# One attention and channel-mix kernel: every engine's order set by hand in place of a scheduler's, with a new start

## The chip, the cores and the metric

The kernel runs on one core of one Trainium2 chip. The profile lists five engines: PE with the matmuls and transposes (1324 instructions in the changed kernel), DVE (385), ACT (229), POOL (57), and SP, for which it shows nothing but transfers being issued. The program gives each engine its own queue of instructions, and the profile tells what an engine waited for. The metric is device time in microseconds (us) of one execution; the executions of one kernel lie within 0.3 to 1.4% of each other. A profiled execution gives a trace; its span, from the first to the last instruction, is about 1.8 us shorter than the time.

## The reference, cut to what matters

```python
# 8 batches, 8 heads, 576 rows, 64 columns a head; C = 512, F = 1024
q_s = softmax(q, over the 64 columns); k_s = softmax(k, over the 576 rows)
kv  = einsum('bhsd,bhse->bhde', k_s, v)
x   = einsum('bhsd,bhde->bhse', q_s, kv)          # to (batch, 576, 512)
x_prev = x shifted by one row
xk = mu_k * x + (1 - mu_k) * x_prev
xr = mu_r * x + (1 - mu_r) * x_prev
out = sigmoid(xr @ w_r) * (relu(xk @ w_k)**2 @ w_v)
```

## The kernel before: the parts that matter

Attention is made per batch in two groups of four heads, so there are 16 groups. The parts of a group, with the names that the profile uses:

```python
exp(i)        # ACT: eqk <- raw, exp of q (i=0) and of k (i=1)
cast_v        # ACT: vv <- raw
norm_q        # DVE: rsum <- eqk, rrec, qs <- eqk * rrec          (about 3.0 us)
kv, weights   # PE: kvp <- vv, eqk;  DVE: rz, w <- kvp * rz
transpose_q   # PE: qtp <- qs, 9 transposes
copy_qt       # ACT: qt <- qtp
x(0), x(1)    # PE: xp <- qt, w;  ACT: xb <- xp
diff          # DVE: xb (first rows), xd
mix(0), mix(1)# DVE: xm, xk;  xm, xr                               (1.4 us each)
```

The two layers are made per pair of batches (1152 rows) in three units of 512, 384 and 256 rows: `kfp` (PE) -> `rel` (ACT) -> square `k` or `k2` (DVE), then per 128 rows `rp` (PE) -> `th` (ACT) and `vp` (PE) -> `ot` (DVE) -> store. A unit can begin only when xk of its last batch is there.

Only the start (batch 0) had its order by hand. From then on a generator laid out attention pieces between matmul groups, and the framework's scheduler put the instructions of PE, ACT and DVE in order:

```python
for pair in range(B // 2):
    for c0, n in UNITS:
        advance(ASTEPS * (2 * pair + (c0 + n - 1) // S))
        for c in unit(pair, c0, n, 4 if pair == 0 and c0 == 0 else 1):
            cols += c
            advance(min((B - 1) * ASTEPS, ASTEPS * (cols + per_batch // 8) // per_batch))
```

The softmax here doesn't subtract the row's maximum and nothing guards it: scores larger than these inputs give would overflow.

Of the kernel before, what the change touches and what calls it, by code (L numbers as in the profile page):

```python
# [18 lines left out]
def kernel(  # L19
# [42 lines left out]
    ctx.enter_context(tc.manual_schedule(engines={mybir.EngineType.Pool}))  # L62

    def emit_load(b: int, g: int, queues=None):
        t = ldpool.tile([128, 3, 2, J * D], F32, tag="raw", name="raw")
        ld = []
        for i, src in enumerate((q, k, v)):
            ap = bass.AP(tensor=src.tensor,
                         offset=src.offset + (b * H + 2 * g) * S * D,
                         ap=[[J * D, 128], [4 * S * D, 2], [1, J * D]])  # L70
            queue = queues[i] if queues else nc.gpsimd
            ld.append(queue.dma_start(out=t[:, i, :, :], in_=ap))  # L72
        raw[b, g] = t
        return ld

    first = emit_load(0, 0, (nc.sync, nc.scalar, nc.sync))
# [5 lines left out]
    emit_load(0, 1, (nc.scalar, nc.sync, nc.scalar))  # L82
# [4 lines left out]

    ident = const.tile([128, 128], BF16, name="ident")
# [20 lines left out]
    def emit_weights(gate):  # L109
# [11 lines left out]
        for u in range(2):  # L121
            part(wr_bf, moe_w_r, C, u, 0, C)
        n = FT // 2
# [16 lines left out]

    class Attention:
        def __init__(self, b: int, g: int):
            self.b, self.g = b, g
            self.t = raw.pop((b, g))
# [8 lines left out]
        def exp(self, i: int):  # L153
            nc.scalar.activation(  # L154
                out=self.eqk[:, i, :, :, :],
                in_=self.t[:, i, :, :].rearrange("p u (j d) -> p j u d", d=D),
                func=ACT.Exp)
# [5 lines left out]
        def norm_q(self):  # L163
# [3 lines left out]
            rrec = apool.tile([128, 2 * J], F32, tag="rrec", name="rrec")  # L167
            nc.vector.reciprocal(out=rrec[:], in_=rsum[:])
# [3 lines left out]
                in1=rrec[:, :, None].to_broadcast((128, 2 * J, D)), op=ALU.mult)  # L172

        def kv(self, tag: str):
# [3 lines left out]
            else:  # L178
                self.kvp = [psum.tile([128, 512], F32, tag="mm", bufs=4, name="kvp")[:, :]
                            for _ in range(2)]  # L180
            for j in range(J):
# [27 lines left out]
        def x(self, hf: int):  # L209
            self.xp = psum.tile([128, 1024], F32, tag="att", bufs=2, name="xp")  # L210
            for c, e in ((0, 8), (8, J)):
                nc.tensor.matmul(self.xp[:, 64 * c:64 * e], lhsT=self.w[:, hf, :],  # L212
                                 rhs=self.qt[:, c:e, 64 * hf:64 * hf + 64],
                                 start=True, stop=True)
            nc.scalar.copy(out=self.xb[:, hf, 64:64 + S], in_=self.xp[:, 0:S])  # L215
# [20 lines left out]
    def attention(b: int, g: int):  # L236
        a = Attention(b, g)
        a.exp(0)
        a.exp(1)
        a.cast_v(nc.scalar.copy)  # L240
        a.norm_q()
        yield
        a.kv("att")
        a.weights()
        yield
        a.transpose_q()
        a.copy_qt()
        yield
        a.x(0)
        yield  # L250
        a.x(1)
        yield
        a.diff()
        a.mix(0)
        yield
        a.mix(1)
        yield


    def unit(pair: int, c0: int, n: int, step: int = 1):  # L260
        xk, xr = xpair[pair]
        k2 = mpool.tile([128, FT, 512], BF16, tag="k2", name="k2")
        for f0 in range(0, FT, step):
            kfps = [psum.tile([128, 512], F32, tag="mm", bufs=4, name="kfp")
                    for _ in range(step)]
            for cts in ((0, 1), (2, 3)) if step > 1 else (range(CT),):
                for i, kfp in enumerate(kfps):
                    fc = f0 + i
                    for ct in cts:
                        nc.tensor.matmul(kfp[:, 0:n],  # L270
                                         lhsT=wk_bf[:, ct, fc * 128:(fc + 1) * 128],
                                         rhs=xk[:, ct, c0:c0 + n],
                                         start=(ct == 0), stop=(ct == CT - 1))
            for i, kfp in enumerate(kfps):
                rel = mpool.tile([128, 512], BF16, tag="rel", bufs=3, name="rel")
                nc.scalar.activation(out=rel[:, 0:n], in_=kfp[:, 0:n], func=ACT.Relu,  # L276
                                     scale=HALF_ROOT)
                nc.vector.tensor_tensor(out=k2[:, f0 + i, 0:n], in0=rel[:, 0:n],
                                        in1=rel[:, 0:n], op=ALU.mult)
                yield n  # L280
        for m in range(n // 128):
            rp = psum.tile([128, C], F32, tag="mm", bufs=4, name="rp")
# [3 lines left out]
            th = mpool.tile([128, C], F32, tag="th", name="th")  # L286
            nc.scalar.activation(out=th[:], in_=rp[:], func=ACT.Tanh, scale=0.5)  # L287
            yield 512
            vp = psum.tile([128, C], F32, tag="mm", bufs=4, name="vp")
            for ft in range(FT):  # L290
                nc.tensor.matmul(vp[:], lhsT=k2[:, ft, 128 * m:128 * m + 128],  # L291
                                 rhs=wv_bf[:, ft, :], start=(ft == 0), stop=(ft == FT - 1))
            ot = opool.tile([128, C], F32, tag="ot", name="ot")
            nc.vector.scalar_tensor_tensor(out=ot[:], in0=th[:], scalar=1.0, in1=vp[:],  # L294
                                           op0=ALU.add, op1=ALU.mult)
            for i in range(2):
# [7 lines left out]
    def drain(gen):  # L304
        for _ in gen:
            pass
# [93 lines left out]
```

## Time and profile before

| | before |
|---|---|
| time, median of 3 (range) | 221.39 us (220.98 to 221.61) |
| span of the profiled execution | 219.7 us |
| first kfp that run through from | 27.82 us |
| ten periods between the groups' transposes, 6th to 16th | 118.9 us, 11.89 each |

The first view gives busy times in stretches of the span. The columns are PE, weight loads, DVE, ACT, POOL, each with its count of instructions, then the granted PE clock (1.00 is full), the share of DMA time, and GB/s. Where the trace has no clock record the clock column is 1.00 too; in this kernel the first record is at 24.27 us, so before that the column tells nothing.

```profile
core 0: us, PE busy (x) PEld busy (x) DVE busy (x) ACT busy (x) POOL busy (x), PEclk, DMA share, GB/s
0.00:28.00 28.00, 9.96 (x72) 5.98 (x73) 12.96 (x38) 12.52 (x14) 11.33 (x22) 0.99 1.03 250
28.00:60.00 32.00, 30.12 (x210) 14.88 (x209) 31.25 (x68) 31.05 (x45) 13.17 (x19) 0.95 1.03 398
60.00:200.00 140.00, 138.25 (x949) 72.53 (x948) 116.33 (x268) 98.49 (x161) 11.30 (x16) 1.00 0.44 140
```

In the first 28 us PE stands 18 us. From 28 to 60 us DVE and ACT are full (31.25 and 31.05 of 32 us). From 60 to 200 us PE is idle for 1.75 of 140 us. The list of waits of PE says for what it stood:

```profile
engine line waited for: us in total, times, longest us
PE mup L134 <- DMA mu_sb<-in_moe_mu_r_dram: 9.8, 1, 9.8
PE kfp L270 <- DVE xk L232: 3.7, 2, 2.9
...
PE kvp L184 <- ACT vv_107 L160: 2.1, 1, 2.1
PE qtp L202 <- DVE qs L170: 1.5, 1, 1.5
...
```

And the timeline shows where the start ends: kfp begin at 20.80 us on the half of xk that is ready, stop, and run on only from 27.82 us. Those at 20.80 us start 0.43 us apart, where 0.22 us is usual from 60 us on: PE ran at half rate there. (Start, duration, engine, line, operation, tile; in brackets the idle time before and what ended it.)

```profile
20.80 2.77 PE L270 MATMUL kfp<-xk,wk_bf 128*128 128x512 bf16 x6
...
24.30 0.59 PE L270 MATMUL kfp<-xk,wk_bf 128*128 128x512 bf16 x2
27.82 2.72 PE L270 MATMUL kfp<-xk,wk_bf 128*128 128x512 bf16 x6 [2.92 <-DVE xk L232]
```

### The profile page before, as it was taken

Reading aid. Unit: us, or ns where it says so; the run is one execution under the profiler, and the core shown is the slowest. Engines: PE = TensorE matmul, PEld = TensorE weight load, DVE = VectorE, ACT = ScalarE, POOL = GpSimd, SP = SyncE. Lnnn points to the kernel's source line nnn. Section 1 sums busy time; section 2 is a strip of 40 time slices with the busy share of each in tenths; the row PEclk is TensorE's granted clock in tenths of the full one; section 3 lists DMA queues with packets and bytes.
Section 4 is the critical chain, followed back from the end, with each engine's and each line's share of the span. In section 5 each row is a group of like instructions: output and inputs, shape, how many; then the busy total and the mean of one; then the engine's idle time right before and its main releaser. Section 6 shows DMA issues by size and latency. Waiting matters only on the chain.

```text
span 219.7 us, 3641 instructions
## 1 busy us (share of the span) xinstructions
PE 193.5 (88%) x1313; PEld 101.6 (46%) x1313; DVE 166.3 (76%) x384; ACT 147.7 (67%) x230; POOL 35.8 (16%) x56
## 2 busy tenths in 40 slices
PE   0156599988999999999999999999999999999991
PEld 0134134534547454445557443546465444554650
DVE  1196389999999998889798998888787758483431
ACT  2645279999977779676929696949736392644340
POOL 1294252433431210230030000000000000000000
PEclk9999969999999999999999999999999999999999
DMA  6999999999999791897085220232131400340414
GB/s 215 397 158 199 262 402 388 393 400 403 404 393 406 273 343 71 256 298 288 3 264 201 49 51 0 57 90 48 36 88 24 95 3 22 73 95 5 108 36 95
DMA packets 16171, 40.62 MB, mean 185 GB/s; under 512 B 2072, under 2 KB 4632, under 8 KB 16152
## 3 DMA queue, kind: packets, MB, share of 16 engines
q0 software_dynamic: 8736, 27.40, 38.0%
q1 hardware_dynamic: 6600, 11.22, 18.0%
q10 hardware_dynamic: 816, 1.77, 2.2%
q8 instruction: 10, 0.16, 0.3%
q14 instruction: 9, 0.07, 0.1%
HBM read 33.56 MB, written 9.44 MB: 196 GB/s over the span
## 4 chain that ended last, share of the span: by engine, by line
PE 60%; ACT 19%; DVE 13%; DMA 3%; issue 2%; SPq 1%; DVEq 0%; ACTq 0%
PE vp L291 22%; PE kfp L270 19%; PE rp L284 11%; ACT eqk L154 5%; ACT qt L207 4%; ACT rel L276 4%; DMA mu_sb<-in_moe_mu_r_dram 3%; PE kvp L184 3%; PE qtp L202 3%; PE xp L212 2%; DVE rsum L166 2%; DVE xk L232 2%; DVE qs L170 2%; ACT xb_105 L215 2%; ACT xb_109 L215 1%
## 5 line engine op out<-in xcount | busy, mean ns | idle before, releaser
L270 PE MATMUL kfp<-xk,wk_bf 128*128 128x384 bf16 (+2 forms) x384 | 72.6, 335 | 4.3 <-DVE xk L232 3.7
L276 ACT ACTIVATE rel<-kfp 128x512 bf16<-128x512 f32 (+2 forms) x96 | 45.4, 518 | 20.5 <-PE kfp L270 19.5
L270 PEld LDWEIGHTS <-wk_bf 128*128 128x128 bf16 x384 | 36.3, 99 | 30.3 <-issue 8.5
L154 ACT ACTIVATE eqk<-raw 128x1152 bf16<-128x1152 f32 x32 | 37.5, 1204 | 9.7 <-DMA raw<-in_q_dram 5.9
L294 DVE SCALAR_TENSOR_TENSOR ot<-th,vp 128x512 f32<-128x512 f32 x36 | 24.6, 683 | 17.3 <-PE vp L291 12.5
L287 ACT ACTIVATE th<-rp 128x512 f32<-128x512 f32 x36 | 22.7, 631 | 21.7 <-PE rp L284 20.7
L284 PE MATMUL rp<-wr_bf,xr 128*128 128x512 bf16 x144 | 37.0, 379 | 0.0
L207 ACT COPY qt<-qtp 128x1152 bf16<-128x1152 bf16 x16 | 18.2, 1136 | 7.7 <-PE qtp L202 7.5
L166 DVE TENSOR_REDUCE rsum<-eqk 128x18 f32<-128x1152 bf16 x16 | 21.6, 1348 | 1.6 <-ACT eqk L154 1.5
L170 DVE TENSOR_TENSOR qs<-eqk,rrec 128x1152 bf16<-128x1152 bf16 x16 | 21.7, 1355 | 0.8
L230 DVE TENSOR_SCALAR xm<-xd,mu 128x576 bf16<-128x576 bf16 x64 | 21.6, 378 | 0.4
L284 PEld LDWEIGHTS <-xr 128*128 128x128 bf16 x144 | 13.3, 98 | 13.8
L72 POOL DMA_DIRECT2D raw<-in_q_dram x14 | 10.0, 713 | 52.9 <-ACT vv_111 L160 24.0
L212 PE MATMUL xp<-qt,w 128*128 128x512 bf16 x64 | 13.5, 302 | 2.6 <-ACT qt L207 2.3
L184 PEld LDWEIGHTS <-eqk 64*128 64x128 bf16 x288 | 9.4, 100 | 9.2 <-issue 8.3
L202 PE MATMUL qtp<-ident,qs 128*128 128x128 bf16 x144 | 11.6, 231 | 1.5 <-DVE qs L170 1.5
L202 PEld LDWEIGHTS <-qs 128*128 128x128 bf16 x144 | 9.8, 103 | 4.1 <-DVE qs L170 1.8
L212 PEld LDWEIGHTS <-w 128*128 128x128 bf16 x64 | 6.3, 103 | 11.0 <-issue 6.1
L72 POOL DMA_DIRECT2D raw<-in_v_dram x14 | 10.0, 711 | 8.4 <-DMA raw<-in_q_dram 5.8
L72 POOL DMA_DIRECT2D raw<-in_k_dram x14 | 10.0, 711 | 5.7 <-DMA raw<-in_v_dram 3.0
L195 DVE SCALAR_TENSOR_TENSOR w<-kvp,rz,mask 128x128 bf16<-128x128 f32 x32 | 9.7, 345 | 0.0
L134 PE MATMUL mup<-identf,mu_sb 8*128 8x8 f32 x1 | 0.2, 243 | 9.8 <-DMA mu_sb<-in_moe_mu_r_dram 9.8
(83 smaller groups left out, 238.7 us busy)
## 6 DMA issues: line engine op xcount, KB each, us to landing
out_dram<-ot SPq DMA_DIRECT2D x72, 128.0 KB, 2.4
raw<-in_q_dram POOLq DMA_DIRECT2D x14, 576.0 KB, 12.4
raw<-in_k_dram POOLq DMA_DIRECT2D x14, 576.0 KB, 12.7
raw<-in_v_dram POOLq DMA_DIRECT2D x14, 576.0 KB, 13.1
wk_bf<-in_moe_w_k_dram POOLq DMA_DIRECT2D x4, 256.0 KB, 6.5
wv_bf<-in_moe_w_v_dram POOLq DMA_DIRECT2D x2, 512.0 KB, 12.4
raw<-in_k_dram ACTq DMA_DIRECT2D x1, 576.0 KB, 5.6
raw<-in_q_dram SPq DMA_DIRECT2D x1, 576.0 KB, 5.2
```

Source lines behind the costliest of these rows:

```text
L72: ld.append(queue.dma_start(out=t[:, i, :, :], in_=ap))
L154: nc.scalar.activation(out=self.eqk[:, i, :, :, :], in_=self.t[:, i, :, :].rearrange("p u (j d) -> p j u d", d=D), func=ACT.Exp)
L166: nc.vector.reduce_sum(out=rsum[:], in_=eq, axis=AX.X)
L170: nc.vector.tensor_tensor(out=self.qs[:].rearrange("p j (u d) -> p (j u) d", u=2), in0=eq, in1=rrec[:, :, None].to_broadcast((128, 2 * J, ...
L202: nc.tensor.transpose(out=self.qtp[:, j, :], in_=self.qs[:, j, :], identity=ident[:])
L207: nc.scalar.copy(out=self.qt[:], in_=self.qtp[:, 0:J, :])
L212: nc.tensor.matmul(self.xp[:, 64 * c:64 * e], lhsT=self.w[:, hf, :], rhs=self.qt[:, c:e, 64 * hf:64 * hf + 64], start=True, stop=True)
L270: nc.tensor.matmul(kfp[:, 0:n], lhsT=wk_bf[:, ct, fc * 128:(fc + 1) * 128], rhs=xk[:, ct, c0:c0 + n], start=(ct == 0), stop=(ct == CT - 1))
L276: nc.scalar.activation(out=rel[:, 0:n], in_=kfp[:, 0:n], func=ACT.Relu, scale=HALF_ROOT)
L284: nc.tensor.matmul(rp[:], lhsT=xr[:, ct, c0 + 128 * m:c0 + 128 * m + 128], rhs=wr_bf[:, ct, :], start=(ct == 0), stop=(ct == CT - 1))
L291: nc.tensor.matmul(vp[:], lhsT=k2[:, ft, 128 * m:128 * m + 128], rhs=wv_bf[:, ft, :], start=(ft == 0), stop=(ft == FT - 1))
L294: nc.vector.scalar_tensor_tensor(out=ot[:], in0=th[:], scalar=1.0, in1=vp[:], op0=ALU.add, op1=ALU.mult)
```

## The change: intent and diff

The idea is to start the layers earlier, to keep PE's clock up from the first microsecond, and to place every instruction of every engine by a plan instead of a scheduler's guess. The plan has a clock of its own, that of PE's work: each matmul group adds a duration that stands in the source (1.71 us for the eight matmuls of one vp; in the trace of the kernel before, eight of them took 1.73 us, from 62.11 to 63.84), and each attention piece is emitted when this clock passes its point.

```diff
 # start: q, k and v of the first group split over two queues, each half by u
+                for u, queue in ((0, nc.sync), (1, nc.scalar)):
+                    ld.append(queue.dma_start(out=t[:, i, u, :], ...))
 # filler matmuls on zeros in front of kv and x of batch 0 (20 + 5 + 4 + 4)
+    def filler(dst, count: int):
+        for _ in range(count):
+            nc.tensor.matmul(dst, lhsT=zeros[:, 0:128], rhs=zeros[:], start=True, stop=True)
 # order of the loads: wk, wr, batch 1, then wv (before: wk, wr, wv, batch 1)
+    a1.cast_v(nc.gpsimd.tensor_copy)     # before: on ACT
+    emit_load(1, 0)
+    emit_load(1, 1)
+    emit_wv()
 ...
+    ctx.enter_context(tc.manual_schedule(engines={E.PE, E.Activation, E.DVE, E.Pool, E.SP}))
 # attention of one group, at points of the plan's clock (second number: PE time)
+        return [
+            (t, 0.0, begin),
+            (t, 0.0, call("exp", 0)),
+            (t + 1.2, 0.0, call("exp", 1)),
+            (t + 1.4, 0.0, call("sum_q")),
+            (t + 2.4, 0.0, call("cast_v", nc.scalar.copy)),
+            (t + 2.4, 0.0, load),
+            (t + 3.0, 0.0, call("norm_q")),
+            (t + 4.4, 0.65, call("kv", "att")),
+            (t + 5.0, 0.65, call("transpose_q")),
+            (t + 5.0, 0.0, call("weights")),
+            (t + 5.7, 0.0, call("copy_qt")),
+            (t + 7.2, 0.33, call("x", 0)),
+            (t + 7.2, 0.33, call("x", 1)),
+            (t + 7.6, 0.0, call("copy_x", 0)),
+            (t + 8.1, 0.0, call("copy_x", 1)),
+            (t + 9.6, 0.0, call("diff")),
+            (t + 10.6, 0.0, call("mix", 0)),
+            (t + 11.8, 0.0, call("mix", 1)),
+        ]
+    BASE = {(1, 0): 5.5, (1, 1): 10.0}
+    for n in range(4, 2 * B):
+        BASE[n // 2, n % 2] = 22.0 + 10.6 * (n - 4)
 ...
+    def attend(last_batch: int):
+        while events and (events[0][0] <= clock or any(e[2] <= last_batch for e in events)):
+            _, _, _, cost, fn = events.pop(0)
+            fn(); clock += cost
 # units: two r groups stand ahead of the v groups; each group's ACT and DVE work
 # is emitted after the attention pieces that have come due in the meantime
```

More of the change, by code (lines that the diff above doesn't have):

```diff
@@ L61, with emit_load @@
     SYNC = mybir.DependencyInfo(mybir.DependencyClass.Sync, mybir.DependencyReason.DATA)
-    ctx.enter_context(tc.manual_schedule(engines={mybir.EngineType.Pool}))
-    def emit_load(b: int, g: int, queues=None):
+    E = mybir.EngineType
+    ctx.enter_context(tc.manual_schedule(engines={E.PE, E.Activation, E.DVE, E.Pool, E.SP}))
+    def emit_load(b: int, g: int):
         t = ldpool.tile([128, 3, 2, J * D], F32, tag="raw", name="raw")
@@ L67, in emit_load @@
         for i, src in enumerate((q, k, v)):
-            ap = bass.AP(tensor=src.tensor,
-                         offset=src.offset + (b * H + 2 * g) * S * D,
-                         ap=[[J * D, 128], [4 * S * D, 2], [1, J * D]])
-            queue = queues[i] if queues else nc.gpsimd
-            ld.append(queue.dma_start(out=t[:, i, :, :], in_=ap))
+            ap = [[J * D, 128], [4 * S * D, 2], [1, J * D]]
+            off = src.offset + (b * H + 2 * g) * S * D
+            if (b, g) != (0, 0):
+                queue = nc.gpsimd if b > 0 else nc.sync
+                ld.append(queue.dma_start(
+                    out=t[:, i, :, :], in_=bass.AP(tensor=src.tensor, offset=off, ap=ap)))
+            else:
+                for u, queue in ((0, nc.sync), (1, nc.scalar)):
+                    ld.append(queue.dma_start(
+                        out=t[:, i, u, :],
+                        in_=bass.AP(tensor=src.tensor, offset=off + 4 * S * D * u,
+                                    ap=[ap[0], ap[2]])))
         raw[b, g] = t
         return ld
-    first = emit_load(0, 0, (nc.sync, nc.scalar, nc.sync))
+    first = emit_load(0, 0)
     mu_sb = const.tile([8, 128], F32, name="mu_sb")
@@ L81 @@
                           in_=ap)
-    emit_load(0, 1, (nc.scalar, nc.sync, nc.scalar))
+    emit_load(0, 1)
     warm = const.tile([1, 1], F32, name="warm")
@@ L85 @@
     nc.scalar.activation(out=warm[:], in_=warm[:], func=ACT.Exp)
+    zeros = const.tile([128, 512], BF16, name="zeros")
+    nc.vector.memset(zeros[:], 0.0)
     ident = const.tile([128, 128], BF16, name="ident")
@@ L107, with emit_wk_wr @@
     wr_bf = const.tile([128, CT, C], BF16, name="wr_bf")
-    def emit_weights(gate):
+    def emit_wk_wr(gate):
         def part(dst, src, n, u, c0, c1):
@@ L122, in emit_weights, with emit_wv @@
             part(wr_bf, moe_w_r, C, u, 0, C)
+    def emit_wv():
         n = FT // 2
@@ L143, in __init__ @@
             self.b, self.g = b, g
+            self.xps = {}
             self.t = raw.pop((b, g))
@@ L153, in exp @@
         def exp(self, i: int):
-            nc.scalar.activation(
+            return nc.scalar.activation(
                 out=self.eqk[:, i, :, :, :],
@@ L161, in cast_v, with sum_q @@
                  in_=self.t[:, 2, :, :].rearrange("p u (j d) -> p j u d", d=D))
-        def norm_q(self):
+        def sum_q(self):
             eq = self.eqk[:, 0, :, :, :].rearrange("p j u d -> p (j u) d")
@@ L166, in norm_q @@
             nc.vector.reduce_sum(out=rsum[:], in_=eq, axis=AX.X)
-            rrec = apool.tile([128, 2 * J], F32, tag="rrec", name="rrec")
-            nc.vector.reciprocal(out=rrec[:], in_=rsum[:])
+            self.rrec = apool.tile([128, 2 * J], F32, tag="rrec", name="rrec")
+            nc.vector.reciprocal(out=self.rrec[:], in_=rsum[:])
+        def norm_q(self):
+            eq = self.eqk[:, 0, :, :, :].rearrange("p j u d -> p (j u) d")
             self.qs = apool.tile([128, J, 128], BF16, tag="qs", name="qs")
@@ L171, in norm_q, with kv @@
                 out=self.qs[:].rearrange("p j (u d) -> p (j u) d", u=2), in0=eq,
-                in1=rrec[:, :, None].to_broadcast((128, 2 * J, D)), op=ALU.mult)
-        def kv(self, tag: str):
+                in1=self.rrec[:, :, None].to_broadcast((128, 2 * J, D)), op=ALU.mult)
+        def kv(self, tag: str, fill: int = 0):
             if tag == "att":
@@ L180, in kv @@
                             for _ in range(2)]
+            filler(self.kvp[0], fill)
             for j in range(J):
@@ L207, in copy_qt, with x, copy_x @@
             nc.scalar.copy(out=self.qt[:], in_=self.qtp[:, 0:J, :])
-        def x(self, hf: int):
-            self.xp = psum.tile([128, 1024], F32, tag="att", bufs=2, name="xp")
+        def x(self, hf: int, fill: int = 0):
+            xp = psum.tile([128, 1024], F32, tag="att", bufs=2, name="xp")
+            self.xps[hf] = xp
+            filler(xp[:, 0:512], fill)
             for c, e in ((0, 8), (8, J)):
-                nc.tensor.matmul(self.xp[:, 64 * c:64 * e], lhsT=self.w[:, hf, :],
+                nc.tensor.matmul(xp[:, 64 * c:64 * e], lhsT=self.w[:, hf, :],
                                  rhs=self.qt[:, c:e, 64 * hf:64 * hf + 64],
                                  start=True, stop=True)
-            nc.scalar.copy(out=self.xb[:, hf, 64:64 + S], in_=self.xp[:, 0:S])
+        def copy_x(self, hf: int):
+            nc.scalar.copy(out=self.xb[:, hf, 64:64 + S], in_=self.xps[hf][:, 0:S])
         def diff(self):
@@ L234, in mix, with unit @@
                 in0=xm[:], in1=self.xb[:, :, 0:S], op=ALU.add)
-    def attention(b: int, g: int):
-        a = Attention(b, g)
-        a.exp(0)
-        a.exp(1)
-        a.cast_v(nc.scalar.copy)
-        a.norm_q()
-        yield
-        a.kv("att")
-        a.weights()
-        yield
-        a.transpose_q()
-        a.copy_qt()
-        yield
-        a.x(0)
-        yield
-        a.x(1)
-        yield
-        a.diff()
-        a.mix(0)
-        yield
-        a.mix(1)
-        yield
-    def unit(pair: int, c0: int, n: int, step: int = 1):
+    def unit(pair: int, c0: int, n: int, group: int):
@@ L261, in unit @@
         xk, xr = xpair[pair]
         k2 = mpool.tile([128, FT, 512], BF16, tag="k2", name="k2")
-        for f0 in range(0, FT, step):
-            kfps = [psum.tile([128, 512], F32, tag="mm", bufs=4, name="kfp")
-                    for _ in range(step)]
-            for cts in ((0, 1), (2, 3)) if step > 1 else (range(CT),):
-                for i, kfp in enumerate(kfps):
-                    fc = f0 + i
-                    for ct in cts:
-                        nc.tensor.matmul(kfp[:, 0:n],
-                                         lhsT=wk_bf[:, ct, fc * 128:(fc + 1) * 128],
-                                         rhs=xk[:, ct, c0:c0 + n],
-                                         start=(ct == 0), stop=(ct == CT - 1))
-            for i, kfp in enumerate(kfps):
-                rel = mpool.tile([128, 512], BF16, tag="rel", bufs=3, name="rel")
-                nc.scalar.activation(out=rel[:, 0:n], in_=kfp[:, 0:n], func=ACT.Relu,
-                                     scale=HALF_ROOT)
-                nc.vector.tensor_tensor(out=k2[:, f0 + i, 0:n], in0=rel[:, 0:n],
-                                        in1=rel[:, 0:n], op=ALU.mult)
-                yield n
@@ L281, in unit, with k_mm, k_post @@
-        for m in range(n // 128):
-            rp = psum.tile([128, C], F32, tag="mm", bufs=4, name="rp")
+        ths = {}
+        def k_mm(kfp, fc, cts):
+            for ct in cts:
+                nc.tensor.matmul(kfp[:, 0:n], lhsT=wk_bf[:, ct, fc * 128:(fc + 1) * 128],
+                                 rhs=xk[:, ct, c0:c0 + n],
+                                 start=(ct == 0), stop=(ct == CT - 1))
+        def k_post(kfp, fc):
+            rel = mpool.tile([128, 512], BF16, tag="rel", bufs=4, name="rel")
+            nc.scalar.activation(out=rel[:, 0:n], in_=kfp[:, 0:n], func=ACT.Relu,
+                                 scale=HALF_ROOT)
+            nc.vector.tensor_tensor(out=k2[:, fc, 0:n], in0=rel[:, 0:n], in1=rel[:, 0:n],
+                                    op=ALU.mult)
@@ L283, in unit, with mm_tile, r_step @@
+        def mm_tile(name):
+            return psum.tile([128, 512], F32, tag="mm", bufs=4, name=name)
+        def r_step(m):
+            rp = mm_tile("rp")
             for ct in range(CT):
@@ L285, in unit, with post, v_step @@
                                  rhs=wr_bf[:, ct, :], start=(ct == 0), stop=(ct == CT - 1))
-            th = mpool.tile([128, C], F32, tag="th", name="th")
-            nc.scalar.activation(out=th[:], in_=rp[:], func=ACT.Tanh, scale=0.5)
-            yield 512
-            vp = psum.tile([128, C], F32, tag="mm", bufs=4, name="vp")
+            def post():
+                ths[m] = mpool.tile([128, C], F32, tag="th", bufs=4, name="th")
+                nc.scalar.activation(out=ths[m][:], in_=rp[:], func=ACT.Tanh, scale=0.5)
+            return post
+        def v_step(m):
+            vp = mm_tile("vp")
             for ft in range(FT):
@@ L292, in unit @@
                                  rhs=wv_bf[:, ft, :], start=(ft == 0), stop=(ft == FT - 1))
-            ot = opool.tile([128, C], F32, tag="ot", name="ot")
-            nc.vector.scalar_tensor_tensor(out=ot[:], in0=th[:], scalar=1.0, in1=vp[:],
-                                           op0=ALU.add, op1=ALU.mult)
-            for i in range(2):
-                jb = (2 * S * pair + c0 + 128 * m) // 64 + i
-                bb, j = jb // J, jb % J
-                dst = bass.AP(tensor=out.tensor, offset=out.offset + (bb * S + j) * C,
-                              ap=[[J * C, 64], [1, C]])
-                nc.sync.dma_start(out=dst, in_=ot[64 * i:64 * i + 64, :])
@@ L302, in unit, with post @@
-            yield 1024
-    def drain(gen):
-        for _ in gen:
-            pass
-    emit_weights(first[2])
+            def post():
+                ot = opool.tile([128, C], F32, tag="ot", name="ot")
+                nc.vector.scalar_tensor_tensor(out=ot[:], in0=ths.pop(m)[:], scalar=1.0,
+                                               in1=vp[:], op0=ALU.add, op1=ALU.mult)
+                for i in range(2):
+                    jb = (2 * S * pair + c0 + 128 * m) // 64 + i
+                    bb, j = jb // J, jb % J
+                    dst = bass.AP(tensor=out.tensor, offset=out.offset + (bb * S + j) * C,
+                                  ap=[[J * C, 64], [1, C]])
+                    nc.sync.dma_start(out=dst, in_=ot[64 * i:64 * i + 64, :])
@@ new lines, in v_step @@
+            return post
+        for f0 in range(0, FT, group):
+            kfps = [mm_tile("kfp") for _ in range(group)]
+            if group > 1:
+                for i, kfp in enumerate(kfps):
+                    k_mm(kfp, f0 + i, range(CT // 2))
+                for i, kfp in enumerate(kfps):
+                    k_mm(kfp, f0 + i, range(CT // 2, CT))
+                    yield n * CT / 2400, (lambda kfp=kfp, fc=f0 + i: k_post(kfp, fc))
+            else:
+                k_mm(kfps[0], f0, range(CT))
+                yield n * CT / 2400, (lambda kfp=kfps[0], fc=f0: k_post(kfp, fc))
@@ new lines, in unit @@
+        tiles = n // 128
+        ahead = tiles if group > 1 else min(2, tiles)
+        for m in range(ahead):
+            yield C * CT / 2400, r_step(m)
+        for m in range(tiles):
+            yield C * FT / 2400, v_step(m)
+            if m + ahead < tiles:
+                yield C * CT / 2400, r_step(m + ahead)
+    emit_wk_wr(first[5])
+    a0 = Attention(0, 0)
+    a1 = Attention(0, 1)
+    a0.exp(0)
+    a0.sum_q()
+    a0.norm_q()
+    a0.exp(1)
+    a0.cast_v(nc.scalar.copy)
+    a0.kv("mm", 20)
@@ L310 @@
+    a0.transpose_q()
+    a0.weights()
+    a1.exp(0)
+    a0.copy_qt()
+    a1.cast_v(nc.gpsimd.tensor_copy)
     emit_load(1, 0)
     emit_load(1, 1)
-    with tc.manual_schedule(engines={mybir.EngineType.PE, mybir.EngineType.DVE,
-                                     mybir.EngineType.Activation}):
-        emit_mu()
-        a0 = Attention(0, 0)
-        a1 = Attention(0, 1)
-        a0.exp(0)
-        a0.exp(1)
-        a0.norm_q()
-        a0.cast_v(nc.scalar.copy)
-        a1.exp(0)
-        a0.kv("mm")
-        a0.transpose_q()
-        a0.copy_qt()
-        a0.weights()
-        a1.exp(1)
-        a1.norm_q()
-        a0.x(0)
-        a0.x(1)
-        a1.cast_v(nc.scalar.copy)
-        a1.kv("mm")
-        a1.transpose_q()
-        a1.copy_qt()
-        a0.diff()
-        a0.mix(0)
-        a1.weights()
-        a1.x(0)
-        a1.x(1)
-        a1.diff()
-        a1.mix(0)
-        a0.mix(1)
-        a1.mix(1)
@@ L344, in attention_of @@
-    def attention_of(batches):
-        for b in batches:
-            for g in range(2):
-                if b + 1 < B:
-                    emit_load(b + 1, g)
-                yield from attention(b, g)
-    ASTEPS = 14
-    att = attention_of(range(1, B))
-    done = 0
-    cols = 0
-    per_batch = S * (FT + CT * 3)
-    def advance(want):
-        nonlocal done
-        while done < want:
-            next(att, None)
-            done += 1
+    emit_wv()
+    a1.exp(1)
+    a1.sum_q()
+    a1.norm_q()
@@ new lines, with pieces, begin, call @@
+    for hf in range(2):
+        a0.x(hf, 5 * (1 - hf))
+        a0.copy_x(hf)
+    emit_mu()
+    a1.kv("mm", 4)
+    a1.transpose_q()
+    a1.copy_qt()
+    a1.weights()
+    a0.diff()
+    a0.mix(0)
+    for hf in range(2):
+        a1.x(hf, 4 * (1 - hf))
+        a1.copy_x(hf)
+    a1.diff()
+    a1.mix(0)
+    a0.mix(1)
+    a1.mix(1)
+    def pieces(t: float, b: int, g: int):
+        box = {}
+        def begin():
+            box["a"] = Attention(b, g)
+            if b + 1 < B:
+                pending_loads.append((b + 1, g))
+        def call(name, *args):
+            return lambda: getattr(box["a"], name)(*args)
+        def load():
+            emit_load(*pending_loads.pop(0)) if pending_loads else None
+        return [
[18 more added lines that the diff above has]
+        ]
@@ new lines @@
+    pending_loads = []
+    events = []
+    BASE = {(1, 0): 5.5, (1, 1): 10.0}
+    for n in range(4, 2 * B):
+        BASE[n // 2, n % 2] = 22.0 + 10.6 * (n - 4)
+    for (b, g), t in BASE.items():
+        for i, (at, cost, fn) in enumerate(pieces(t, b, g)):
+            events.append((at, len(events), b, cost, fn))
+    events.sort()
+    clock = 0.0
+    def attend(last_batch: int):
+        nonlocal clock
+        while events and (events[0][0] <= clock or
+                          any(e[2] <= last_batch for e in events)):
+            _, _, _, cost, fn = events.pop(0)
+            fn()
+            clock += cost
@@ L363 @@
     for pair in range(B // 2):
         for c0, n in UNITS:
-            advance(ASTEPS * (2 * pair + (c0 + n - 1) // S))
-            for c in unit(pair, c0, n, 4 if pair == 0 and c0 == 0 else 1):
-                cols += c
-                advance(min((B - 1) * ASTEPS, ASTEPS * (cols + per_batch // 8) // per_batch))
-    drain(att)
+            attend(2 * pair + (c0 + n - 1) // S)
+            for dur, post in unit(pair, c0, n, 4 if pair == 0 and c0 == 0 else 1):
+                clock += dur
+                attend(-1)
+                post()
```

## The prediction

> **What bounds the kernel now.** Three phases, by windows and timeline.
>
> 1. Start, 0 to 27.8 us. First-layer matmuls (kfp) run through only from 27.82 us, after PE waited 2.92 us for DVE's xk. Before that PE stands (list of waits): 9.8 us for the loads, 2.1 us for ACT's v cast, 1.5 us for qs, 2.3 us in all for qt. q and k of group 0 land at about 6 us, v at 9.4, group 1 at 9.5 to 12.7.
> 2. 28 to 58 us. ACT and DVE are busy 5.00 of nearly every 5 us, and the chain of waits from 36 us on runs on ACT: batch 1's q lands only at 28.95 us (wk, wr and wv are loaded ahead of it), then exps of batches 1 and 2 push Relu and Tanh back. [...]from 25 to 35 us the granted clock was 0.77 and 0.89.
> 3. 60 to 215 us. PE-bound: [...] The tail is 5 us. [...]
>
> **What the change does.**
> - First loads are split over two queues, so q lands first: estimate 4.6, k 6.1, v 7.6 us (0.59 MB each at the 397 GB/s of 5 to 10 us). Group 0 moves 1.3 to 1.8 us forward.
> - Group 1's v cast goes from ACT (1.17 us) to POOL[...]. POOL issues batch 1's loads after it.
> - Diff and mix of group 0 queue behind weights of group 1 on DVE. I expect kfp to begin at 20 us and to run through from about 22.8 us: gain 5 us, the largest part.
> - The 33 fillers (0.22 us warm) lie in PE's idle time: free, and the clock should be 1.0 from 15 us on, worth under 1 us.
> - wv (2 MB, 5 us) goes behind batch 1, whose q then lands near 22 us. wv lands near 35 us, just when the first vp wants it: a stall of 0 to 2 us is possible.
> - Attention comes at 10.6 us of PE's clock per group. Per group DVE needs about 7.1 us for attention and 2.9 for the layers: 10.0 of PE's 10.4 us; ACT 9.4. [...]From 45 to 170 us both engines are nearly full and strictly in order, so small stalls stay; then PE runs alone.
>
> **Sum (estimate).** [...]tail 4.7, stalls 4: 210 us span; + 1.7 between span and time = 211.5 us. PE carries the critical path throughout.
>
> Range 206 to 217 us. Faster by over 2%: 0.88; within 2%: 0.09; slower: 0.03.
>
> **Right if** unbroken kfp starts at 21 to 24 us, the clock stays 1.0 after 15 us, ACT is no longer 100% busy from 30 to 60 us and the chain there lies on PE, DVE stays at 95% or more from 45 to 165 us, and PE waits on DVE (xk, k2, ot) in small pieces.
>
> **Wrong if** the POOL cast takes 4 us or more or slows DVE; wk competes with group 1's loads; wv is late; or DVE at 97% gives long stalls at unit starts (xk): then the result nears 217.

A term of the sum is missing, PE's work left from 22.8 us on: the sum began at 22.8 us, and this term, the tail of 4.7 and the stalls of 4 brought it to 210 us of span and 211.5 us of time.

## The result, and the profile after

The changed kernel is correct and takes 239.19 us (median of 4, 238.39 to 240.83); the kernel before, with the run made beside it, 221.23 us (median of 4, 220.98 to 221.61). The ratio is 1.082, 95% interval 1.076 to 1.088: 8% slower. The view has the same columns as the first one:

```profile
0.00:28.00 28.00, 22.33 (x132) 10.30 (x135) 18.50 (x49) 15.80 (x21) 14.10 (x24) 1.00 1.02 299
28.00:60.00 32.00, 25.46 (x183) 13.20 (x185) 23.95 (x52) 21.33 (x32) 8.52 (x12) 0.95 1.00 340
60.00:200.00 140.00, 120.68 (x837) 64.93 (x848) 109.85 (x248) 95.36 (x149) 14.83 (x21) 0.96 0.43 136
```

The start did get better: PE's idle time up to 28 us falls from 18.0 to 5.7 us (10.6 us of the busy time are fillers), and PE runs at full rate: the kfp at 21.74 us below start 0.22 us apart. The loss is later. From 28 to 60 us PE is idle for 6.5 instead of 1.9 us, and from 60 to 200 us for 19.3 instead of 1.75 us, at a mean clock of 0.96. DVE is busy for 109.85 of 140 us there, 78%, and ACT for 68%: no engine is full. What PE waits for is mainly one thing:

```profile
PE qtp L224 <- DVE qs L191: 17.9, 13, 2.0
PE kfp L271 <- DVE xk L258: 5.0, 3, 3.3
PE vp L299 <- DVE k L279: 1.6, 2, 1.1
PE kvp L206 <- POOL vv L178: 1.3, 1, 1.3
...
```

The timeline shows the start's gain: the kfp that run through begin at 21.74 us, not 27.82.

```profile
19.06 1.89 PE L271 MATMUL kfp<-xk,wk_bf 128*128 128x512 bf16 x7 [0.85 <-DVE xk L258]
21.74 5.34 PE L271 MATMUL kfp<-xk,wk_bf 128*128 128x512 bf16 x24 [0.80 <-DVE xk L258]
```

The next view is the chain of waits of the changed kernel between 122 and 137 us: what each step was released by, in order of time (start, duration, what; "issue" is time for which the view names no wait).

```profile
122.01 1.28 DVE qs L191
...
123.33 0.69 PE qtp L224 x9
...
124.05 1.13 ACT qt L229
...
125.84 0.70 DVE ot L304
...
126.55 0.17 ACT xb L241
...
127.08 0.41 ACT rel L277
...
127.52 0.29 DVE k L279
...
127.95 0.76 DVE xd L247
...
129.11 0.57 DVE xm L256 x2
...
129.71 0.76 DVE xk L258
...
131.07 0.57 DVE xm L256 x2
...
131.66 0.76 DVE xr L258
...
132.62 1.27 DVE rsum L184
...
134.33 1.27 DVE qs L191
...
135.65 0.68 PE qtp L224 x9
```

Lines that are left out are under 0.7 us each. It goes from the end of one group's qs (123.29) to the end of the next group's qs (135.60), 12.3 us, and PE's only own part in it is 0.69 us of transposes. Every link needs the one before or stands behind it in the same queue: PE transposes qs of group n, ACT copies it to qt, PE makes x (at 125.57 us by the timeline, in an "issue" piece that is left out), ACT copies x to xb, DVE makes xd, xm and xk, xm and xr of group n. Only then does DVE's queue come to rsum and qs of group n+1, and PE's queue stands at the transposes of group n+1. So the chain closes on itself. I call it the loop. Of the 12.3 us, adding up all the view's lines, DVE has 8.7 (6.35 of attention, 0.70 of ot and 1.63 of squares that stand in between), ACT 1.7, PE 0.7, and 1.2 are "issue". (The ot at 125.84 us is no link of its own: by the timeline x on PE, 125.57 to 126.22, and its two copies on ACT, 126.02 to 127.20, ran in the same time.)

The period between the transposes of the 6th and the 16th group is 12.83 us on average (68.28 to 196.59 us, ten periods), 11.89 before, and 10.6 of PE's clock were planned. (The first four of the ten take 13.0 to 14.3 us; they hold three stretches of 3.4 us at half clock. The last six take 12.2 on average. The expectations of e2b and e7 count from the 5th group on: 12.76 us, and 11.46 for e1.) The kernel before has no such loop: its scheduler ran q's work far ahead. Its 14th qs ended at 130.9 us and the transposes that read it began at 163.3 us, 32 us later. In the changed kernel the 14th qs ended at 172.50 us and its transposes began at 172.56; the distance is 0.1 us or less for every group from the 5th to the 16th.

The three engines worked in the order of their queues; the changed kernel's trace shows it at these places. PE stood idle for 1.27 us before the transposes at 123.33 us, while seven vp, which ran right after them without a wait, stood behind them in its queue. ACT stood idle for 3.49 us before the qt at 124.05 us; behind it, at 127.88 us, stood an exp of the next group, whose q had been on its way since 105.40 us (the loads issued from 90 to 130 us landed 4.3 to 7.8 us after their issue). DVE stood idle for 1.70 us before rz of the second group at 15.76 us; behind it, at 16.49 us, stood the first group's diff, whose x had been copied by 14.05 us.

### The profile page after: what moved, and what is told of

The parts are those of the page before. It is cut to its first block, busy times and chain, and to the rows that moved or that the text cites. A ratio compares the mean times of both kernels' runs of the same rounds, so it can differ in the third digit from the quotient of the medians.

```text
span 239.0 us, 3672 instructions
## 1 busy us (share of the span) xinstructions
PE 202.4 (85%) x1324; PEld 106.0 (44%) x1346; DVE 168.6 (71%) x385; ACT 147.4 (62%) x229; POOL 37.4 (16%) x57
## 4 chain that ended last, share of the span: by engine, by line
DVE 37%; PE 35%; DMA 12%; ACT 7%; issue 5%; POOL 1%; ACTq 0%; DVEq 0%; POOLq 0%
PE vp L299 13%; PE kfp L271 11%; DVE qs L191 7%; DMA wv_bf<-in_moe_w_v_dram 6%; DVE rsum L184 6%; DVE xm L256 6%; PE rp L288 5%; DVE ot L304 4%; PE qtp L224 4%; DVE k L279 4%; DMA wr_bf<-in_moe_w_r_dram 4%; DVE xk L258 3%; DVE xd L247 3%; DVE xr L258 3%; ACT xb L241 3%
## 5 line engine op out<-in xcount | busy, mean ns | idle before, releaser
L271 PE MATMUL kfp<-xk,wk_bf 128*128 128x384 bf16 (+2 forms) x380 | 70.3, 340 | 5.3 <-DVE xk L258 5.0
L299 PE MATMUL vp<-wv_bf,k 128*128 128x512 bf16 x281 | 67.4, 384 | 2.5 <-DVE k L279 1.6
L271 PEld LDWEIGHTS <-wk_bf 128*128 128x128 bf16 x384 | 38.5, 102 | 33.2 <-issue 8.9
L279 DVE TENSOR_TENSOR k<-rel 128x512 bf16<-128x512 bf16 (+2 forms) x96 | 32.3, 352 | 23.5 <-ACT rel L277 21.8
L299 PEld LDWEIGHTS <-k 128*128 128x128 bf16 x288 | 28.1, 99 | 36.5 <-issue 2.7
L304 DVE SCALAR_TENSOR_TENSOR ot<-th,vp 128x512 f32<-128x512 f32 x36 | 24.3, 676 | 25.2 <-PE vp L299 12.3
L229 ACT COPY qt<-qtp 128x1152 bf16<-128x1152 bf16 x16 | 17.9, 1117 | 38.6 <-PE qtp L224 38.6
L288 PE MATMUL rp<-wr_bf,xr 128*128 128x512 bf16 x134 | 35.3, 385 | 1.2 <-ACT rel L277 0.6
L224 PE MATMUL qtp<-ident,qs 128*128 128x128 bf16 x144 | 11.7, 231 | 17.9 <-DVE qs L191 17.9
L241 ACT CAST xb<-xp 128x576 bf16<-128x576 f32 x32 | 19.2, 646 | 8.5 <-PE xp L236 8.5
L178 ACT CAST vv<-raw 128x1152 bf16<-128x1152 f32 x15 | 17.5, 1167 | 0.5 <-DMA raw<-in_v_dram 0.5
L206 PE MATMUL kvp<-vv,eqk 64*128 64x129 bf16 x288 | 11.2, 218 | 2.5 <-POOL vv L178 1.3
L258 DVE TENSOR_TENSOR xr<-xm,xb 128x1152 bf16<-128x1152 bf16 x16 | 12.1, 759 | 0.6
```

Of the source, the lines that this page charges most:

```text
L224: nc.tensor.transpose(out=self.qtp[:, j, :], in_=self.qs[:, j, :], identity=ident[:])
L258: nc.vector.tensor_tensor(out=xpair[self.b // 2][m][:, 2 * g:2 * g + 2, c0:c0 + S], in0=xm[:], in1=self.xb[:, :, 0:S], op=ALU.add)
L271: nc.tensor.matmul(kfp[:, 0:n], lhsT=wk_bf[:, ct, fc * 128:(fc + 1) * 128], rhs=xk[:, ct, c0:c0 + n], start=(ct == 0), stop=(ct == CT - 1))
L279: nc.vector.tensor_tensor(out=k2[:, fc, 0:n], in0=rel[:, 0:n], in1=rel[:, 0:n], op=ALU.mult)
L288: nc.tensor.matmul(rp[:], lhsT=xr[:, ct, c0 + 128 * m:c0 + 128 * m + 128], rhs=wr_bf[:, ct, :], start=(ct == 0), stop=(ct == CT - 1))
L299: nc.tensor.matmul(vp[:], lhsT=k2[:, ft, 128 * m:128 * m + 128], rhs=wv_bf[:, ft, :], start=(ft == 0), stop=(ft == FT - 1))
```

## The experiments

All kernels give correct results. Edits are against the changed kernel, unless told otherwise. Times are medians; ratios are to the kernel before.

| run | edit | time, us | ratio (95%) | PE waits for qs, us | period, us |
|---|---|---|---|---|---|
| changed kernel | | 239.19 | 1.082 (1.076 to 1.088) | 17.9 | 12.83 |
| e4 | changed start, scheduled main loop | 222.67 | 1.0051 (1.0026 to 1.0076) | | |
| e5 | start of before, changed main loop | 243.78 | 1.1021 (1.0951 to 1.1092) | 19.4 | 12.67 |
| e11 | without fillers | 240.71 | 1.0849 (1.0812 to 1.0886) | 18.7 | 12.70 |
| e6 | attention every 11.4 instead of 10.6 | 232.83 | 1.0536 (1.0494 to 1.0577) | 12.7 | 12.77 |
| e2, e2b | mix(1) behind next qs | 226.27 | 1.0202 (1.0166 to 1.0238) | 6.9 | 11.51 |
| e3 | mix(0) and mix(1) behind next qs | 245.09 | 1.1053 (1.0989 to 1.1117) | 5.3 | 12.98 |
| e1 | next rsum and qs before diff | 228.94 | 1.0349 (1.0319 to 1.0378) | 1.2 | 11.60 |
| e7 | e1, every 11.4 | 246.54 | 1.1148 (1.1096 to 1.1201) | 1.2 | 13.98 |
| e8 | e7, batch 1 earlier, others later | 243.36 | 1.0998 (1.0978 to 1.1019) | 1.2 | 14.10 |
| e9 | next rsum and qs right behind w | 221.60 | 0.9992 (0.9973 to 1.0011) | 1.2 | 10.76 |
| e10 | e9, all attention earlier | 218.06 | 0.9834 (0.9809 to 0.9860) | 1.2 | 11.12 |

The 1.2 us of the last rows is one wait in the start. Theory A is the loop; theory B is that DVE simply has too much work per group.

### Which half loses: the start or the main loop (e4, e5, e11)

e4 is the kernel before with the changed start. Against the kernel before:

```diff
-    first = emit_load(0, 0, (nc.sync, nc.scalar, nc.sync))
+    first = emit_load(0, 0)               # halves of q, k, v on two queues
-        a1.cast_v(nc.scalar.copy)
+        a1.cast_v(nc.gpsimd.tensor_copy)  # and fillers, order of batch 0, wv behind batch 1
```

> The changed kernel's start (split loads, order by hand, fillers, v cast on POOL, wv behind batch 1) with the main loop of the kernel before, whose order the scheduler sets. If the start's gain of 6 us (unbroken kfp at 21.7 instead of 27.8 us) is real and carries to the end: 212 to 217 us. If the scheduled main loop gives it back (it was bound by ACT and by late loads there): 218 to 222 us. Both theories of the main loop agree here; a time near 239 would put the loss into the start.

222.67 us, 0.7 us above the second range and far from 239: the loss is not in the start, but the gain is gone too. The timeline shows where PE stood. The scheduler put kv of batch 1 ahead of the layers' second half on PE's queue, and PE stood 7.16 us for the cast of batch 1's v:

```profile
19.06 1.89 PE L298 MATMUL kfp<-xk,wk_bf 128*128 128x512 bf16 x8 [0.85 <-DVE xk L257]
28.10 1.16 PE L205 MATMUL kvp<-vv,eqk 64*128 64x129 bf16 x18 [7.16 <-ACT vv L177]
...
30.02 1.49 PE L298 MATMUL kfp<-xk,wk_bf 128*128 128x512 bf16 x3
```

e5 is the other half alone:

```diff
-    first = emit_load(0, 0)                       # split loads, fillers, v cast on POOL
+    first = emit_load(0, 0, (nc.sync, nc.scalar, nc.sync))
 ...                                               # start's order as before; wv ahead of batch 1
```

> The start of the kernel before (whole loads, no fillers, v cast on ACT, wv ahead of batch 1, same order by hand) with the changed main loop: the other half of the change alone. If the changed main loop is the loss and the changed start a gain of about 6 us inside it, the time is 242 to 248 us, and the transposes wait about 18 us for qs as in the changed kernel. If the fillers or the split loads caused the loss, it falls to near 221 us.

243.78 us, with 19.4 us of waits for qs. So the main loop is the whole loss, and inside it the start is worth 4.6 us (243.78 less 239.19).

e11 takes the fillers away:

```diff
-    a0.kv("mm", 20)
+    a0.kv("mm", 0)              # and so for a1.kv and both x
```

> The changed kernel without its 33 filler matmuls on zeros, nothing else. If they only keep the clock up in PE's idle time, kvp and qtp of the start run cold again (1.16 instead of 0.70 us for 18 kvp) and the first kfps too: 0.5 to 2 us slower, 239.5 to 241.5 us. If they stand in the way (each x waits for its 4 or 5 fillers), it is 0 to 1 us faster.

240.71 us, inside the range of the first answer. By the medians the fillers are worth 1.5 us, but the two intervals overlap, so that they shorten the whole is not shown. The traces show that PE's rate in the start is higher with them: up to 28 us a kvp lasts 308 ns on average without them and 217 with them, a kfp of 512 columns 448 and 379 ns, and PE has come to 29 kfp without them, to 31 kfp and 6 rp with them.

### A loop or too much work (e6, e2, e3, e1)

e6 changes one number:

```diff
-        BASE[n // 2, n % 2] = 22.0 + 10.6 * (n - 4)
+        BASE[n // 2, n % 2] = 22.0 + 11.4 * (n - 4)
```

> The changed kernel with attention spread wider: 11.4 instead of 10.6 us of PE's clock per group, nothing else. Theory A (a cycle of 12.8 us through the queues): the cycle is still longer than 11.4, so the measured period stays at 12 us or more and the time above 233 us. Theory B (DVE too full at 10.6): the load per us falls by 7%, the waits go, and the time falls to 225 us or less.

PE's waits for the transposes are 12.7 us in twelve:

```profile
PE qtp L224 <- DVE qs L191: 12.7, 12, 1.5
...
```

The period did not move: 12.77 us against 12.83, though 0.8 us more were planned. That is what a loop does whose length doesn't depend on the plan. The time fell all the same to 232.83 us, just under theory A's bound and far above B's. The last transposes begin at 197.3 us (196.6 in the changed kernel), so attention takes as long as there; but with more of the layers planned beside each group, PE waits less in each period (12.7 us for qs in all) and has less left to do when attention is over. I had not thought of that when I set 233 as the bound.

That spacing alone could not have mended the order is an estimate, not a run. Adding up the plan's own numbers, a pair of batches costs 46.2 us of PE's clock (38.4 for the layers, 4 times 1.96 for the groups), so a group must come every 11.6 us on average. A loop of 12.8 us is longer than that.

e2 and e3 take links out of the loop:

```diff
-            (t + 10.6, 0.0, call("mix", 0)),      # e3 only
-            (t + 11.8, 0.0, call("mix", 1)),      # e2 and e3
+            (t + 13.7, 0.0, call("mix", 0)),
+            (t + 13.8, 0.0, call("mix", 1)),
```

> The changed kernel, but mix(1) of a group (1.4 us on DVE) is put behind qs of the next group: one link taken out of the supposed cycle. Theory A: the period falls by about 1.4 us to 11.4, 12 groups times 1.4 are 16 us: 222 to 227 us. Theory B (DVE load): no change, 236 us or more.

226.27 us: as theory A had it. One of the four executions took 1147 us, and it was the profiled one; it is left out. In its trace a vp matmul lasts 1705 ns on average (384 in the changed kernel) while the clock column is 1.00; the cause is not known. So the kernel was run once more for its profile:

> The mix(1)-late kernel once more, for a profile (that of its first run was spoilt by an execution of 1147 us). Loop theory: waits for qs fall from 17.9 to under 9 us and the period between transposes from 12.76 to 11.3 to 11.8 us; time 225 to 227 us as timed before.

227.43 us in one execution (state unknown), waits for qs 6.9 us, period 11.51 us: it fell by 1.3 us for 1.4 us of DVE work taken out of the loop.

> As before, but mix(0) and mix(1) both go behind qs of the next group: 2.8 us out of the cycle. Theory A: the cycle is then shorter than the planned 10.6 us, waits for qs fall to under 4 us, 209 to 218 us; xk comes later, which can cost some us at unit starts. Theory B: no change, 236 us or more.

245.09 us, 6 us slower than the changed kernel. Here my count of the loop was too simple. Waits for qs did fall to 5.3 us, but two others came:

```profile
PE kfp L271 <- DVE xk L258: 14.2, 5, 5.3
PE xp L236 <- DVE w L217: 7.7, 7, 2.3
PE qtp L224 <- DVE qs L191: 5.3, 6, 1.2
...
```

The mixes moved from in front of qs to in front of w (DVE's queue then holds qs, xm, xk, xm, xr, rz, w), and x needs w as much as it needs the transposed q. From w through x, xb, xd, rsum, qs and both mixes to the next w is again one round through all of DVE's attention work. The period was 12.98 us on average. Two of the ten, 17.2 and 15.9 us, hold waits for xk of 3.6 and 3.7 us, so the average is not the loop alone; but the last seven are still 12.0 us on average, though 2.8 us were taken out. xk came later against the unit that reads it: 14.2 us of waits in all. A link is out of a loop only if no other path closes it.

e1 turns the order around, for batches from 2 on:

```diff
+        Q = 4.2 if b > 1 else 0.0
-            (t, 0.0, call("exp", 0)),
-            (t + 1.4, 0.0, call("sum_q")),
-            (t + 3.0, 0.0, call("norm_q")),
+            (t - Q, 0.0, call("exp", 0)),
+            (t + 1.4 - Q, 0.0, call("sum_q")),
+            (t + 3.0 - Q, 0.0, call("norm_q")),
```

> The changed kernel, but from batch 2 on exp of q, the row sums and the normalised q (qs) of a group are put 4.2 us of PE's clock earlier, so that on DVE they stand before diff and mix of the group before. Same work, same density of attention. Theory A (a cycle through the in-order queues: qs of group n, PE transposes, ACT copy, PE x, ACT copies, DVE diff and mixes, and only then rsum and qs of group n+1; it takes about 12.8 us per group where 10.6 are planned): the cycle is cut, PE's waits for qs (17.9 us) all but vanish, the period between transposes falls to 10.5 to 11 us, time 208 to 216 us. Theory B (DVE has too much work per group, or the 10.6 us are too dense for it): only the order of the same work is changed, so the time stays above 230 us.

228.94 us. The waits for qs are gone (1.2 us), the time is 10 us better with the same work, which theory B did not allow; but the period is 11.60 us, not 10.5 to 11, and the time 13 us above my range. PE now waited for xk (7.2 us), for squares (3.8) and for less at several places: the old loop was cut, and the order was still not good.

### The rest: where q's work stands, and how late the attention is (e7 to e10)

e7 adds e6's spacing to e1:

```diff
-        BASE[n // 2, n % 2] = 22.0 + 10.6 * (n - 4)     # with e1's Q
+        BASE[n // 2, n % 2] = 22.0 + 11.4 * (n - 4)
```

> The kernel with q's work ahead of diff and mix (228.9 us) and the wider spacing of 11.4 us. There the period was 11.46 us for 10.6 planned with waits for k2 and xk left. If these are what DVE at nearly full load costs once the cycle is cut, 11.4 us of spacing removes them: 219 to 224 us. If another cycle is left that the spacing doesn't touch: 227 us or more.

246.54 us, 18 us worse than e1, in the range of the second answer; that a further loop is the reason is not shown. PE's waits for xk rose to 15.7 us, at the units' starts. One of them:

```profile
100.40 1.35 DVE L184 TENSOR_REDUCE rsum<-eqk 128x18 f32<-128x1152 bf16 x1 [1.90 <-ACT eqk L172]
...
102.31 0.49 PE L271 MATMUL kfp<-xk,wk_bf 128*128 128x384 bf16 x2
...
102.73 0.76 DVE L247 TENSOR_TENSOR xd<-xb 128x1152 bf16<-128x1152 bf16 x1
103.41 1.35 DVE L191 TENSOR_TENSOR qs<-eqk,rrec 128x1152 bf16<-128x1152 bf16 x1
...
105.35 0.76 DVE L258 TENSOR_TENSOR xk<-xm,xb 128x1152 bf16<-128x1152 bf16 x1
...
106.17 1.12 PE L271 MATMUL kfp<-xk,wk_bf 128*128 128x384 bf16 x3 [3.37 <-DVE xk L258]
```

kfp of a unit start at 102.31 us, find the second half of xk missing and stand for 3.37 us. On DVE, qs of the next group (1.35 us) stands between xd and the mix of the urgent group. Rsum of the next group, which had waited 1.90 us for its exp, cost little: it ended at 101.75 us, and the copies of x that xd reads ended at 101.71. So x itself was late. Spacing groups wider makes each batch later against the unit that reads it. Adding up the plan's numbers, mix(0) of batches 3, 5 and 7 is planned 0.4, 1.1 and 1.7 us of PE's clock before their units in e7 (I call this their margin), and 2.8, 8.6 and 10.5 us in the changed kernel. Lateness alone is not enough: e6 has the same margins as e7, with q's work behind the mixes, and waits 6.7 us for xk. Nor is q's work ahead enough by itself: e1 has the margins of the changed kernel and waits 7.2 us. Only both together gave 15.7 us.

e8 starts batch 1 earlier, but the later groups later; against e7:

```diff
-    BASE = {(1, 0): 5.5, (1, 1): 10.0}
+    BASE = {(1, 0): 2.5, (1, 1): 7.0}
-        BASE[n // 2, n % 2] = 22.0 + 11.4 * (n - 4)
+        BASE[n // 2, n % 2] = 23.0 + 11.4 * (n - 4)
```

> As the run before, and batch 1's two groups begin 3 us of PE's clock earlier (2.5 and 7.0), the later groups 1 us later. In the q-ahead run PE stood 4.8 us at the second unit's start for batch 1's xk, whose row sums had stood behind all eight squares on DVE and whose exps behind six Relus on ACT. If that order is the cause, the wait falls to 1 to 2 us: 215 to 221 us. If batch 1's loads are the cause, nothing is gained against the run before.

243.36 us. The wait at the second unit is gone from the trace (4.83 us at 50.86 us in e7), so that part held; the time is far above 215 to 221 us. I had moved the later groups the wrong way: their margins are now -0.6, 0.1 and 0.7 us, the longest wait for xk is 6.7 us, and the sum 18.6 us.

e9 goes back to the changed kernel's spacing and puts q's work where DVE has nothing else of the attention to do: right behind w, while PE and ACT make x.

```diff
+        Q = ((0.0, 1.4, 3.0) if b == 1 else (-4.2, -2.8, -1.2) if (b, g) == (2, 0)
+             else (-8.0, -5.2, -4.0))
+            (t + Q[0], 0.0, call("exp", 0)),      # and so sum_q at t + Q[1], norm_q at t + Q[2]
```

> The changed kernel with its spacing of 10.6, but q's work moved further ahead than in the q-ahead run (exp 8.0, row sums and qs 6.6 to 7.0 us of PE's clock, so that row sums and qs of the next group stand on DVE right behind w of this one, in the hole while PE and ACT make x). The loop from w to w is then: row sums and qs 2.9, diff 1.0, two mixes 2.8, w 0.9 us, with x and its copies beside it: about 7.6 us of DVE plus the layers' 2.9, so 10.5 of the 10.6 planned. If the loop theory holds, the period is 10.7 to 11.3 us, waits for qs about 1 us, and the time 220 to 228 us, not above the q-ahead run's 228.9. If the gain of the q-ahead run came from something else (an exp less ahead of a copy, say), it is lost: above 230 us.

221.60 us, 17.6 us better than the changed kernel, with a period of 10.76 us for 10.6 planned, and PE's waits for qs are one, in the start. All as the loop theory said. The list of waits, and the same part of the timeline as the chain above, DVE only, from one w to the next diff:

```profile
PE qtp L224 <- DVE qs L191: 1.2, 1, 1.2
...
124.65 0.61 DVE L217 SCALAR_TENSOR_TENSOR w<-kvp,rz,mask 128x128 bf16<-128x128 f32 x2
125.17 1.34 DVE L184 TENSOR_REDUCE rsum<-eqk 128x18 f32<-128x1152 bf16 x1
...
127.28 1.34 DVE L191 TENSOR_TENSOR qs<-eqk,rrec 128x1152 bf16<-128x1152 bf16 x1
...
129.36 0.76 DVE L247 TENSOR_TENSOR xd<-xb 128x1152 bf16<-128x1152 bf16 x1
```

rsum and qs of the next group (125.17 and 127.28) now fill the time in which PE and ACT make x of this one, and xd follows at 129.36. The 14th qs ended 6.1 us before its transposes began, not 0.06.

```profile
28.00:60.00 32.00, 23.95 (x176) 12.37 (x174) 23.67 (x51) 21.23 (x31) 8.72 (x13) 0.89 0.94 313
60.00:200.00 140.00, 137.92 (x961) 73.43 (x960) 119.53 (x274) 106.20 (x169) 14.83 (x21) 1.00 0.48 151
```

From 60 to 200 us PE is idle for 2.1 instead of 19.3 us, the clock is 1.00 and DVE is at 85%. But from 28 to 60 us it is idle for 8.1 us, 4.8 of them before the second unit, for batch 1's xk.

e10 moves all attention earlier; against e9:

```diff
-    BASE = {(1, 0): 5.5, (1, 1): 10.0}
+    BASE = {(1, 0): 2.5, (1, 1): 7.0}
-        BASE[n // 2, n % 2] = 22.0 + 10.6 * (n - 4)
+        BASE[n // 2, n % 2] = 20.0 + 10.8 * (n - 4)
```

Its margins for batches 3, 5 and 7 are 4.2, 9.2 and 10.3 us.

> As the run before, with the attention earlier against the units that need it: batch 1 at 2.5 and 7.0 instead of 5.5 and 10.0, the later groups from 20.0 on at 10.8. The wide-spaced q-ahead runs (246.5 and 243.4 us) lost 15.7 and 18.6 us waiting for xk at unit starts. If these waits are lateness against the unit starts, they fall to under 6 us here and the time to 214 to 222 us. If they come from q's work standing ahead of the urgent mix on DVE, whatever the start, they stay above 10 us and the time above 228 us.

218.06 us: 1.7% faster than the kernel before, clear of the noise but less than the 2% that is called faster here, and 21 us better than the changed one. PE waits 2.9 us for xk in all. How much of the gain on e9 is the earlier start and how much the spacing of 10.8 was not separated.

```profile
28.00:60.00 32.00, 27.54 (x201) 14.20 (x200) 28.60 (x63) 24.69 (x38) 8.67 (x13) 1.00 1.04 361
60.00:200.00 140.00, 136.36 (x952) 72.87 (x951) 114.49 (x264) 101.63 (x163) 14.83 (x21) 1.00 0.45 140
```

From 28 to 60 us PE's idle time is down to 4.5 us. It is the best kernel found here. Its largest waits left are for qt (3.9 us in five) and for xk; whether placing x later would take them away was not tried.

## Why the prediction was wrong

The prediction had 211.5 us (206 to 217) and 0.88 for faster; it was 239.19 us, 8% slower.

- **The start: right.** It had the unbroken kfp at 21 to 24 us; it was 21.74. exp of the first q began at 4.91 us (estimate for q: 4.6). The v cast on POOL took 1.69 us at 13.30; DVE's qs that ran partly beside it, at 12.62 us, took 1.36 us like the one at 7.80 us. wv came when vp wanted it: one wait of 0.6 us.
- **The step that failed** is the sentence "From 45 to 170 us both engines are nearly full and strictly in order, so small stalls stay", and with it "stalls 4" in the sum. It took 10.0 us of DVE's work in 10.4 us of PE's as proof that a group fits. The load was right: 109.85 us of DVE in 140 us at a period of 12.83 us are 10.07 us a group. But a load only bounds the period from below. The order makes a loop of 12.3 to 12.8 us through five changes of engine, and the period can't be shorter than the longer of the two. In place of "stalls 4" PE waited 17.9 us for qs, and in place of "PE carries the critical path throughout" DVE had 37% of the chain that ended last and PE 35% (by the profile's page; 13 and 60% in the kernel before). The links were all to be read from the old trace: transposes 0.67, qt 1.12, x 0.65, copies 1.2, xb and xd 0.96, two mixes 2.8, rsum, rrec and qs 3.0 make 10.4 us before any square, ot or Relu stands in between. I did not add them up.
- **Phase 2 (28 to 60 us): half right.** ACT is no longer full (21.3 of 32 us), but the chain did not move to PE, and PE's idle time rose by 4.7 us. 3.3 us of its 6.5 are one wait for batch 1's xk at 47.65 us; with batch 1 begun earlier (e10) they are 4.5.
- **The clock: right in the start, wrong after it.** It was to be 1.0 from 15 us on; by the starts of the kfp (0.22 us apart at 21.74 us) it was full there, but it was 0.95 from 28 to 60 us and 0.96 from 60 to 200. In e9 and e10, which have no loop, it is 1.00 from 60 to 200 us. In the changed kernel it was 0.50 from 96 to 98 us, after 4 us (92 to 96) in which PE was busy for 1.9 us and the longest gap was 1.94 us, and 0.50 from 109.35 to 112.7 us, after 4.35 us in which PE was busy for 2.4 us and the longest gap was 1.95 us. What sets it is not shown.
- **DVE at 95% from 45 to 165 us: wrong,** 76% (91.4 of 120 us). The warning that "DVE at 97% gives long stalls at unit starts" named the wrong cause: waits for xk at unit starts were 5.0 us, those for qs 17.9.
- **The account.** The start brings kfp 6.1 us forward (4.6 us of time, by e5). From 28 to 60 us PE's idle time grows by 4.7 us, from 60 to 200 us by 17.6 us, and a clock of 0.96 over 140 us up to 5.6 us more. That is 22 to 28 us lost against 4.6 to 6.1 gained; the spans differ by 19.3 us. The clock's share is the part known least well.

## What to carry to other kernels

When you fix the order of several in-order engines by hand, follow one item's chain until it comes back to the engine and the queue where it began, and add up the durations: if that round is longer than the period you planned, wider spacing and free engines will not shorten the period (e6), and no engine will look full (here PE was busy 86%, DVE 78% and ACT 68% from 60 to 200 us, at a period of 12.83 us; e9 does the same work at 10.76). Break the round by placing work that needs only early inputs (here row sums and q's scaling of the next group) in front of the part that waits, where the engine would stand anyway; moving a link elsewhere in the same round may only close it by another path. Then check each item's margin against its reader, because work that is put ahead can make urgent work late.
